# Fillers of TensorE's waits made of 288-column products of zeros, and a new table of due times, in attention followed by two gated MLPs

## The chip, the cores and the metric

The kernel runs on one core of one Trainium2 chip. The metric is the device time of one execution in microseconds (us); the number that counts is the median of the runs timed without the profiler.

## What is computed

Attention over (4, 8, 576, 64) inputs with a window of 32 keys (heads 0 to 3: the last 32 positions; heads 4 to 7: every fourth of the last 128), then a gated MLP with an RMS norm ahead of it, then a second gated MLP. The weights of the MLPs are 512 x 1536 and 1536 x 512.

```python
attn_out = _attn_ref(q, k, v)                       # masked softmax, 4 x 8 heads, 576 positions
x = attn_out.transpose(0, 2, 1, 3).reshape(2304, 512)
xn = x / sqrt(mean(x * x, -1) + 1e-6) * rms_g       # first MLP
x = (silu(xn @ w_gate) * (xn @ w_val)) @ w_out
gate = 1 / (1 + exp(-(x @ w_gate2)))                # second MLP
return (gate * (x @ w_val2)) @ w_out2
```

## The kernel before

**Products.** Every float32 operand of the MLPs is split into two fp32r halves, "hi" and "lo" (`split`, lines 563 to 574), and each product is three TensorE products (hi hi, hi lo, lo hi). The first MLP (`mlp_step` and `y_group`, lines 1264 and 1306) runs over 7 chunks of tokens, `SIZES` = 288 four times and 384 three times, in three passes over the hidden columns. The second MLP (`unit` and `y_products`, lines 1526 and 1444) works on 2 x 2 blocks with seven products in place of eight; VectorE (DVE) and POOL make the sums and differences of blocks.

**Attention.** 48 groups of three 64-query blocks (`attn_group`). A group is: scores on TensorE (line 918, products on quarters of the array), mask and minimum on DVE (line 930), exponentials on ACT (line 936), reciprocal on DVE, a scaling by it on POOL, DVE or ACT, three transposes on TensorE (line 963), a copy, the product with the values (line 976, again on quarters), a copy into `xT`. Twelve groups have to be done ahead of the first chunk; the others are put between the products of the first MLP's first pass. `x_norm` makes the norm of a chunk: squares on ACT, a sum over partitions with `ones` (line 1039), a Newton iteration on DVE or POOL, a copy `rb` on DVE (line 1080), three transposes of it on TensorE (line 1095, `rbp`), the scaling on DVE (line 1107, `xn`), and the split into `xo`. Of chunk 0 all of this lies ahead of the first MLP product.

**Weights.** The inputs hold float64 weights as pairs of 32-bit words. `words` (lines 525 to 561) turns a 128 x 512 block into float32: one ACT instruction into a tile `wz` (line 546), four on DVE (lines 549, 552, 555 and 558). `wz` has 2 buffers. A weight used later is written from `wz` to DRAM (`weight_ahead`, the transfers `z<-wz`) and loaded again when it is due; the buffer is free when that transfer has landed. ACT works in the order given, so an instruction of line 546 that waits for a buffer holds up all of ACT's work behind it.

**The order.** Nothing runs as the code is written. Every piece of work is added to a list with a cost, an engine (or several that may do it) and a due time, and `Line.emit` plays them against a model of the engines: each engine takes the operation that can start first, ties going to the earlier due time. The due times and costs come from the table `PARAMS` (some 120 numbers). The order of instructions on each engine is what the planner writes down; times on the chip may differ from its model.

**Fillers.** Where the planner's model has TensorE wait for more than `fill_from` (0.52 us) ahead of an operation that carries a `fill`, up to a planned time of 330 us, it puts transposes of the identity, 128 columns each, into the bank that the operation will write (`filler`, line 727), as many as its model of TensorE's clock says fit, less `fill_gap`. Their results are never read. At the very start, `warm_up` (line 798) issues 27 products of a tile of zeros with 288 columns. The model of the clock is in `clocked` and `window_at`, with the levels `low` and `high`; products on quarters of the array cost the planner a switch into and out of that mode, and `stay` is what it adds to an operation that would leave it.

## Time and profile before

| | |
|---|---|
| median of 3 runs, not profiled | 1030.18 us (1029.41 to 1032.03) |
| profiled execution, its own time | 1040.96 us |
| its span, first to last instruction | 1039.2 us |
| TensorE (PE) busy | 1001.9 us, 96% |
| DVE busy | 762.0 us, 73% |
| ACT busy | 497.8 us, 48% |
| POOL busy | 381.4 us, 37% |
| mean granted clock of TensorE | 0.978 of 2.4 GHz |

All times in views of the trace are from the start of the span of the profiled execution. "Busy" of TensorE counts from a product's start to its modelled end, so it says little about how well TensorE is used; where products follow each other, the distance from start to start is what one takes. The granted clock has two levels in the records, 1.00 (2.4 GHz) and 0.50 (1.2 GHz); a value between is a stretch with both.

### The profile page before, as it was taken

How to read it: one execution, taken by the hardware profiler on the slowest of the kernel's cores; microseconds unless marked ns; L12 is line 12 of the kernel's file. 1: busy time of each engine (PE TensorE's matmuls, PEld its weight loads, DVE VectorE, ACT ScalarE, POOL GpSimd, SP SyncE). 2: the span in 40 equal slices, each digit the busy share in tenths (PEclk: the TensorE clock that was granted, in tenths of full speed). 3: DMA queues.
4: the chain of work that ended last, by engine and by line, in shares of the span. 5: the costliest groups of instructions: out<-in, count | busy, mean ns of one | idle time of the engine just before them, and what ended most of it. 6: DMA issues, size and time to landing. Idle time of an engine off the chain costs nothing.

```text
span 1039.2 us, 21287 instructions
## 1 busy us (share of the span) xinstructions
PE 1001.9 (96%) x7586; PEld 964.6 (93%) x7586; DVE 762.0 (73%) x1792; ACT 497.8 (48%) x1380; POOL 381.4 (37%) x550
## 2 busy tenths in 40 slices
PE   7989999999999999999999999998999999999997
PEld 6778989899999999999999988998999999999996
DVE  5879877879877677886544576768986679876765
ACT  4848667654553233432322344656653355544432
POOL 4346742545551101301200463426652146632220
PEclk9769999999999999999999999999999999999999
DMA  8749586756889898888876745436254553267642
GB/s 194 169 102 221 128 249 138 165 191 237 296 313 325 313 321 301 276 296 313 287 275 226 248 150 193 176 122 236 74 199 165 226 225 132 100 205 232 173 97 48
DMA packets 207689, 216.62 MB, mean 208 GB/s; under 512 B 136608, under 2 KB 163808, under 8 KB 207584
## 3 DMA queue, kind: packets, MB, share of 16 engines
q1 hardware_dynamic: 207584, 215.27, 64.3%
q8 instruction: 60, 0.98, 0.4%
q14 instruction: 45, 0.37, 0.1%
HBM read 145.23 MB, written 69.99 MB: 207 GB/s over the span
## 4 chain that ended last, share of the span: by engine, by line
PE 66%; DVE 14%; DMA 8%; ACT 4%; issue 4%; POOL 3%; SPq 1%; DVEq 0%; POOLq 0%; ACTq 0%
PE y L1444 11%; PE v L1264 11%; PE y L1306 10%; PE g L1264 10%; PE att L1526 7%; PE v L1526 6%; PE g L1526 4%; DMA xs<-xs 2%; DMA z<-wz 2%; DVE t L1143 2%; PE att L918 2%; DMA wz<-z 2%; POOL w L569 1%; DVE t L1542 1%; DVE S L645 1%
## 5 line engine op out<-in xcount | busy, mean ns | idle before, releaser
L569 POOL TENSOR_TENSOR h<-t,h 128x288 fp32r<-128x288 f32 (+1 forms) x161 | 148.7, 930 | 382.4 <-ACT h L565 350.7
L565 ACT CAST h<-t 128x288 fp32r<-128x288 f32 (+1 forms) x252 | 110.9, 444 | 169.2 <-DVE t L1287 88.0
L1306 PE MATMUL y<-h,wo 128*128 128x288 f32 (+1 forms) x1008 | 174.2, 318 | 0.1
L1264 PE MATMUL g<-xo,w 128*128 128x288 f32 (+1 forms) x1008 | 169.6, 316 | 1.6 <-ACT t L1278 0.5
L1264 PE MATMUL v<-xo,w 128*128 128x288 f32 (+1 forms) x1008 | 167.8, 315 | 0.0
L1444 PE MATMUL y<-h,wo 128*128 128x288 f32 x1008 | 156.0, 297 | 4.9 <-ACT h L565 1.9
L1264 PEld LDWEIGHTS g<-xo,w 128*128 128x128 f32 x1008 | 156.5, 190 | 3.7 <-DVE t L1283 1.0
L1306 PEld LDWEIGHTS y<-h,wo 128*128 128x128 f32 x1008 | 156.2, 190 | 2.8 <-ACT pt L1326 0.2
L1264 PEld LDWEIGHTS v<-xo,w 128*128 128x128 f32 x1008 | 155.6, 190 | 0.8 <-DVE t L1287 0.2
L1444 PEld LDWEIGHTS y<-h,wo 128*128 128x128 f32 x1008 | 141.4, 189 | 7.6 <-ACT h L565 3.0
L1397 DVE SCALAR_TENSOR_TENSOR pt<-y,pt 128x288 f32<-128x288 f32 x136 | 61.5, 453 | 43.5 <-PE y L1444 40.7
L1287 DVE TENSOR_TENSOR t<-t,v 128x288 f32<-128x288 f32 (+1 forms) x84 | 41.3, 491 | 56.7 <-PE v L1264 52.6
L546 ACT ACTIVATE wz<-wst 128x512 f32<-128x512 f32 x72 | 48.1, 669 | 46.4 <-DMA z<-wz 39.5
L1542 DVE TENSOR_TENSOR t<-t,att 128x288 f32<-128x288 f32 x96 | 43.0, 448 | 31.4 <-PE att L1526 28.0
L549 DVE TENSOR_SCALAR wz<-wz 128x512 f32<-128x512 f32 x72 | 35.6, 494 | 39.4 <-ACT wz L546 38.8
L936 ACT ACTIVATE pr<-pr,nmx 128x96 f32<-128x96 f32 x144 | 52.5, 366 | 20.2 <-DVE nmx L930 19.7
L572 DVE TENSOR_TENSOR h<-t,h 128x288 fp32r<-128x288 f32 (+1 forms) x91 | 50.5, 561 | 13.8 <-ACT h L565 11.7
L555 DVE SCALAR_TENSOR_TENSOR wz<-wst,wz 128x512 int32<-128x512 int32 x72 | 57.7, 803 | 1.9
L558 DVE SCALAR_TENSOR_TENSOR wz<-wst,wz 128x512 int32<-128x512 int32 x72 | 58.0, 806 | 1.4
L1278 ACT ACTIVATE t<-g 128x288 f32<-128x288 f32 (+1 forms) x56 | 24.9, 445 | 70.2 <-PE g L1264 70.1
L1526 PE MATMUL att<-xo,w 128*128 128x288 f32 x336 | 54.0, 296 | 1.0 <-DVE t L1143 0.6
L1526 PE MATMUL att<-wst,w 128*128 128x288 f32 x336 | 54.5, 297 | 0.4 <-ACT t L1536 0.4
(210 smaller groups left out, 1787.0 us busy)
## 6 DMA issues: line engine op xcount, KB each, us to landing
z<-wz SPq DMA_DIRECT2D x60, 256.0 KB, 4.5
xo<-xs SPq DMA_DIRECT2D x23, 576.0 KB, 6.8
wst<-in_moe_w_gate_dram SPq DMA_DIRECT2D x24, 512.0 KB, 5.3
wst<-in_moe_w_val_dram SPq DMA_DIRECT2D x24, 512.0 KB, 6.8
wst<-in_moe_w_out_dram SPq DMA_DIRECT2D x24, 512.0 KB, 5.9
xs<-xs SPq DMA_DIRECT2D x21, 576.0 KB, 5.2
wst<-xs SPq DMA_DIRECT2D x18, 576.0 KB, 6.4
xo<-x SPq DMA_DIRECT2D x16, 576.0 KB, 5.4
```

Source lines behind the costliest of these rows:

```text
L555: add("DVE", Shared(0.595), lambda: nc.vector.scalar_tensor_tensor(out=z.t, in0=top(), scalar=-0x40000000, in1=z.t, op0=ALU.bitwise_and, o ...
L558: add("DVE", Shared(0.595), lambda: nc.vector.scalar_tensor_tensor(out=z.t, in0=low(), scalar=29, in1=z.t, op0=ALU.logical_shift_right, op ...
L565: add("ACT", act(n), lambda: nc.scalar.copy(out=hi(), in_=src()), reads=reads, writes=[key] + [order] * bool(order), tiles=tiles + [dst], ...
L569: add("PL", pool(n), lambda: nc.gpsimd.tensor_tensor(out=lo(), in0=src(), in1=hi().bitcast(F32), op=ALU.subtract), reads=reads, writes=[ke ...
L572: other=(kind + "_lo", "DVE", dves(n), lambda: nc.vector.tensor_tensor(out=lo(), in0=src(), in1=hi().bitcast(F32), op=ALU.subtract)))
L936: add("ACT", PARAMS["exp_cost"], lambda u=u: nc.scalar.activation(out=pr.t[:, u], in_=pr.t[:, u], func=ACTF.Exp, bias=nmx.t[:, u:u + 1], s ...
L1264: nc.tensor.matmul(out=bank.t, lhsT=w[:, l, cols], rhs=x[:, r, j], start=kk == 0 and n == 0, stop=kk == KD - 1 and n == 2)
L1306: nc.tensor.matmul(out=yb.t, lhsT=w.t[:, l, s], rhs=h.t[:, r], start=n == 0 and j == 0, stop=n == HOLDS[p] - 1 and j == 2)
L1397: add("DVE", dve(T), lambda: nc.vector.scalar_tensor_tensor(out=t.t[:, e, h], in0=bank.t, scalar=0.5, in1=t.t[:, e, h], op0=ALU.mult, op1= ...
L1444: nc.tensor.matmul(out=bank.t, lhsT=w.t[:, u, a, n], rhs=hs[u].t[:, d], start=first and u == 0 and m == 0, stop=u == NF // 2 - 1 and m == ...
L1526: nc.tensor.matmul(out=bank.t, lhsT=l.t[:, a, cols], rhs=r.t[:, d, j], start=first and j == 0 and m == 0, stop=j == 1 and m == 2, skip_gro ...
L1542: add("DVE", dve(T), lambda: nc.vector.tensor_tensor(out=t.t, in0=t.t, in1=bank.t, op=ALU.add), reads=[(key, uk)], writes=[ck[name]], tile ...
```

## The change

- The filler is now a product of zeros, `[128 x rows]` by `[128 x n]`, with n the columns of the bank it writes, at most 288. The zeros have a tile of their own in the attention stage's memory, used by `warm_up` too.
- Fillers go in until the attention stage's memory is given up (`SWAP`) and no longer until a planned time; `fill_from` is negative, so the length of a wait no longer keeps fillers out: as many whole ones go in as the planned wait less 0.077 us holds.
- A second rule would add fillers without a wait, where the columns of the last stretch are fewer than a share `fill_share`. The table sets that share to -1.645, so that the lack is below zero everywhere and the rule adds nothing.
- `low` and `high` are 0: the planner's model has TensorE at full clock from its first stretch on.
- `wz` has 3 buffers in place of 2; the second MLP's third home for the same blocks, a tile `z` in the later memory, goes, so there are three there as before.
- Nearly all other numbers of the table are new (`stay` from 0 to 0.699 among them), and with them the order on every engine. `late` changes nothing at these sizes.

The diff, the table cut to the lines that are spoken of:

```diff
 PARAMS = {
...
+    "late": 0, "fill_share": -1.645, "fill_max": 6, "gather": -3.359, "w0_hi": 0.17,
...
-    "xb_zero": -1.298, "stay": 0.0, "phase": 1.6, "fill_to": 330.0, "fill_from": 0.52,
+    "stay": 0.699, "phase": 1.6, "fill_from": -2.118, "fill_gap": 0.077, "margin": 2922.227,
...
@@ emit
-            if o.eng == "PE" and o.fill and start < PARAMS["fill_to"]:
+            if o.eng == "PE" and o.fill and not swapped:
                 begin = free["PE"]
...
-                if begin > self.writer["ident"].end and start - begin > PARAMS["fill_from"]:
-                    while True:
-                        self.window_at(int((begin + PARAMS["phase"]) // 3.4133))
-                        step = 0.083 if self.warm else 0.166
-                        if begin + step > start - PARAMS["fill_gap"]:
-                            break
-                        self.clocked(begin, 0.083, 128)
-                        begin += step
-                        o.fills += 1
+                if begin > self.writer["warm"].end:
...
+                    _, step, size = o.fill
+                    gap = start - begin - PARAMS["fill_gap"]
+                    if start - begin > PARAMS["fill_from"]:
+                        o.fills = max(0, int(gap / step))
+                    o.fills += max(0, min(int(lack / size) - o.fills, int(PARAMS["fill_max"])))
...
@@ words
-        z = new("bp", "z", [P, CW], I32, 1) if late else new("sb", "wz", [P, CW], I32, 2)
+        z = new("bp", "z", [P, CW], I32, 1) if late else new("sb", "wz", [P, CW], I32, 3)
...
-    Z_HOMES = (("sb", "wz", 2),) + (("bp", "z", 1),) * (L2P == ONE)
+    Z_HOMES = (("sb", "wz", 3),)
...
@@ filler
+        size = 1
+        for n in bank.shape[1:]:
+            size *= n
+        size = min(size, T)
...
-                nc.tensor.transpose(t[0:rows, 0:P], ident[:, 0:rows], ident)
+                nc.tensor.matmul(out=t[0:rows, 0:size], lhsT=zeros[:, 0:rows],
+                                 rhs=zeros[:, 0:size], start=True, stop=True)
...
+        return fill, 0.0101 + 0.000425 * size, size
```

How the change moves instructions, at three places. In each line stand the line of the kernel (of the changed one: 14 to 16 higher), the operation, the tile written and the tiles read, the shape, and how many follow each other.

TensorE around the norm of chunk 0, ahead of the first MLP product (`y` is here a bank that the attention borrows; `rb` the norm's copy). Before:

```order
L918 MATMUL att<-kT,qT 64x96 x6
L1039 MATMUL v<-ones,pt 96x1 x3
L918 MATMUL att<-kT,qT 64x96 x12
L727 MATMUL y_1144<-ident 128x128 x35
L1095 MATMUL y_1144<-ident,rb 128x96 x3
L1039 MATMUL att<-ones,pt 96x1 x3
L963 MATMUL att<-ident,pr 96x128 x3
L1264 MATMUL g<-xo,w 128x288 x6
```

The same place now:

```order
L932 MATMUL att<-kT,qT 64x96 x12
L1053 MATMUL v<-ones,pt 96x1 x3
L741 MATMUL y_1181<-zeros 128x288 x30
L1109 MATMUL y_1181<-ident,rb 128x96 x3
L1053 MATMUL att<-ones,pt 96x1 x3
L977 MATMUL att<-ident,pr 96x128 x3
L741 MATMUL att<-zeros 128x192 x3
L990 MATMUL att<-pts,v 64x64 x6
L1278 MATMUL g<-xo,w 128x288 x6
L977 MATMUL att<-ident,pr 96x128 x3
L741 MATMUL att<-zeros 128x192 x10
```

30 products of 288 columns stand where 35 transposes of 128 stood, and 13 shorter ones are new around the first MLP product. In all there are 96 fillers for 58: 73 of 288 columns and 23 of 192, all but one of them ahead of the second half of the first MLP product.

ACT at the program's start (`wst` a loaded weight block, `wz` the tile it goes to, `w` the split halves). Before:

```order
L546 ACTIVATE wz<-wst 128x512 x2
L565 CAST w<-wz 128x256 x2
L779 COPY kT<-v 128x288
L779 COPY kT<-g 128x288
L565 CAST w<-wz 128x256
L546 ACTIVATE wz<-wst 128x512
```

Now:

```order
L553 ACT_TABLE_LOAD
L553 ACTIVATE wz<-wst 128x512 x3
L572 CAST w<-wz 128x256 x2
L795 COPY kT<-v 128x288
L795 COPY kT<-g 128x288
L572 CAST w<-wz 128x256 x2
```

The third block no longer stands behind the first block's split: with three buffers its instruction has one of its own.

TensorE in the first pass of the first MLP, third chunk (scores and values, the products on quarters of the array, are the rows with `kT,qT` and with `pts,v`). Before:

```order
L1264 MATMUL g<-xo,w 128x288 x12
L963 MATMUL att<-ident,pr 96x128 x6
L1264 MATMUL v<-xo,w 128x288 x12
L976 MATMUL att<-pts,v 64x64 x6
L918 MATMUL att<-kT,qT 64x96 x6
L1306 MATMUL y_2598<-h,wo 128x288 x3
L918 MATMUL att<-kT,qT 64x96 x12
L1306 MATMUL y_2633<-h,wo 128x288 x3
L1306 MATMUL y_2652<-h,wo 128x288 x3
L976 MATMUL att<-pts,v 64x64 x6
L1306 MATMUL y_2660<-h,wo 128x288 x3
```

Now:

```order
L1278 MATMUL g<-xo,w 128x288 x12
L932 MATMUL att<-kT,qT 64x96 x18
L990 MATMUL att<-pts,v 64x64 x6
L1278 MATMUL v<-xo,w 128x288 x12
L990 MATMUL att<-pts,v 64x64 x6
L977 MATMUL att<-ident,pr 96x128 x3
L1320 MATMUL y_2756<-h,wo 128x288 x3
L977 MATMUL att<-ident,pr 96x128 x3
L1320 MATMUL y_2761<-h,wo 128x288 x3
L990 MATMUL att<-pts,v 64x64 x12
L1320 MATMUL y_2770<-h,wo 128x288 x3
```

The scores of three groups follow each other where there were one and two. From the first MLP product on, TensorE goes over to products on quarters of the array 29 times in place of 47; the scores stand in 14 unbroken pieces in place of 29, the values in 26 in place of 30. The count of products other than fillers is the same.

On the other engines, counted over the whole program: 30 of the subtractions that make the "lo" halves of weights go from DVE to POOL, 14 of the copies that make the "hi" halves from ACT to DVE, and of the 144 scalings by the reciprocal ACT does 52 in place of 15 (DVE 44 for 70, POOL 48 for 59). In the second MLP's last unit the output products (line 1444) now stand one by one between the products of line 1526, where 28 rows of three followed each other.

## Rows read from the trace of the kernel before

**Rows 1.** Busy time and granted clock by stretch: engines' busy us (instructions), PEclk, DMA share, GB/s.

```profile
40.00:60.00 20.00, 20.00 (x188) 16.75 (x187) 13.17 (x59) 13.49 (x48) 5.77 (x12) 0.50 0.43 116
60.00:80.00 20.00, 16.09 (x115) 14.14 (x114) 16.16 (x52) 10.26 (x39) 9.14 (x22) 0.76 0.64 137
80.00:100.00 20.00, 20.00 (x211) 17.59 (x210) 19.79 (x68) 16.41 (x61) 13.47 (x22) 0.92 0.91 208
140.00:160.00 20.00, 17.62 (x172) 15.86 (x172) 14.60 (x58) 13.08 (x49) 7.64 (x13) 0.91 0.85 240
180.00:200.00 20.00, 19.10 (x201) 17.63 (x202) 17.93 (x54) 12.26 (x46) 10.30 (x26) 0.91 0.66 129
```

**Rows 2.** Chain that ended last, from 83 to 200 us: start us, us, what.

```profile
135.59 7.25 DMA z<-wz
142.86 0.67 ACT wz L546
```

**Rows 3.** TensorE in order of time: start us, us, instruction, count [idle before <-releaser].

```profile
145.33 0.71 PE L918 MATMUL att<-kT,qT 64*64 64x96 f32 x12 [0.74 <-DVE xn L1107]
...
148.96 0.71 PE L918 MATMUL att<-kT,qT 64*64 64x96 f32 x12 [0.72 <-DVE nmx L930]
...
151.67 1.22 PE L918 MATMUL att<-kT,qT 64*64 64x96 f32 x12 [0.90 <-DVE nmx L930]
```

**Rows 4.** TensorE in order of time, without waits, at full clock.

```profile
160.60 0.92 PE L976 MATMUL att<-pts,v 96*64 96x64 f32 x24
161.45 0.66 PE L1306 MATMUL y<-h,wo 128*128 128x288 f32 x3
162.04 1.21 PE L918 MATMUL att<-kT,qT 64*64 64x96 f32 x24
163.18 0.65 PE L1306 MATMUL y<-h,wo 128*128 128x288 f32 x3
...
164.50 0.71 PE L918 MATMUL att<-kT,qT 64*64 64x96 f32 x12
165.15 0.57 PE L976 MATMUL att<-pts,v 96*64 96x64 f32 x12
165.65 0.66 PE L1306 MATMUL y<-h,wo 128*128 128x288 f32 x3
166.15 1.75 PE L1264 MATMUL g<-xo,w 128*128 128x288 f32 x12
167.74 0.81 PE L963 MATMUL att<-ident,pr 128*96 128x128 f32 x6
```

**Rows 5.** TensorE in order of time, the fillers ahead of the norm's transposes.

```profile
58.79 5.89 PE L727 MATMUL y<-ident 128*128 128x128 f32 x35
64.51 0.41 PE L1095 MATMUL y<-ident,rb 96*128 96x96 f32 x3
```

**Rows 6.** DVE in order of time, the norm's copy and the first scaling.

```profile
60.25 0.55 DVE L1080 COPY rb<-rsy 96x384 f32<-96x384 f32 x1
...
64.97 0.94 DVE L1107 SCALAR_TENSOR_TENSOR xn<-xT,gam,y 128x288 f32<-128x288 f32 x2 [3.32 <-PE y L1095]
```

**Rows 7.** Busy time and granted clock of one stretch inside the fillers.

```profile
62.00:64.00 2.00, 2.00 (x18) 2.00 (x17) 0.00 (x0) 0.51 (x4) 0.24 (x1) 0.84 0.80 128
```

**Rows 8.** TensorE in order of time, twelve MLP products at half clock.

```profile
79.26 3.25 PE L1264 MATMUL g<-xo,w 128*128 128x288 f32 x12 [0.43 <-DVE t L1283]
82.44 1.01 PE L918 MATMUL att<-kT,qT 64*64 64x96 f32 x12
```

**Rows 9.** TensorE's waits from 320 us on: us in total, times, longest us.

```profile
PE g L1526 <- DVE t L1542: 6.5, 9, 1.6
PE y L1444 <- POOL h L569: 1.8, 3, 1.0
```

**Rows 10.** TensorE in order of time, a wait in the last unit.

```profile
1010.60 1.06 PE L1526 MATMUL g<-xq,w 128*128 128x288 f32 x6 [0.55 <-DVE t L1542]
```

**Rows 11.** TensorE in order of time, the norm's sums over partitions.

```profile
35.76 1.18 PE L1039 MATMUL v<-ones,pt 128*96 128x1 f32 x12
```

More of the change, by code (lines that the diff above doesn't have):

```diff
@@ new lines @@
+    "w0_lo": 1.905, "h0_hi": 0.438, "h0_lo": 1.239, "x0_hi": 1.34, "x0_lo": 11.623, "ahead": 2,
+    "todo0": 56.796, "todo1": 25.362, "todo2": 159.576, "todo3": 11.023, "xb_zero": 1.288,
+    "stay": 0.699, "phase": 1.6, "fill_from": -2.118, "fill_gap": 0.077, "margin": 2922.227,
+    "wait": 1.059, "w_sq": 42.802, "w_hi": 0.161, "w_lo": 1.285, "x_hi": 1.845, "x_lo": 0.0,
+    "h_hi": 1.711, "h_lo": 0.003, "qk": 1.905, "norm": 0.0, "pts": 18.659, "o": 0.0, "snap": 7.898,
+    "h_ahead": 98.614, "h2_ahead": -0.542, "evac": 0.038, "holds": (4, 4, 4), "norm_act": 0.0,
@@ L45 @@
+    "warm_due": 37.022, "mask_cost": 0.18, "exp_cost": 0.36, "s_cost": 0.546, "o_cost": 0.41,
+    "t_cost": 0.265, "pt_lead": 1.847, "x_lead": 29.885, "wy_due": 1.584, "y_from": 5.448,
+    "y_step": 0.787, "xb_due": -0.013, "y_last": 1.205, "xb_last": 0.798, "lo6": 114.943,
+    "hi6": 132.108, "sizes": (288, 288, 288, 288, 384, 384, 384),
 }
@@ L192, in emit @@
         todo = len(self.ops)
-        picks, watch, stale = {}, {}, set(ready)
+        picks, watch, stale, streamed, swapped = {}, {}, set(ready), [], False
         def choose(eng):
@@ L258, in emit @@
                         begin = max(begin, t.ring.free_at() + PARAMS["cross"])
-                if begin > self.writer["ident"].end and start - begin > PARAMS["fill_from"]:
-                    while True:
-                        self.window_at(int((begin + PARAMS["phase"]) // 3.4133))
-                        step = 0.083 if self.warm else 0.166
-                        if begin + step > start - PARAMS["fill_gap"]:
-                            break
-                        self.clocked(begin, 0.083, 128)
-                        begin += step
-                        o.fills += 1
+                if begin > self.writer["warm"].end:
+                    since = start - 3.4133
+                    streamed = [x for x in streamed if x[1] > since]
+                    lack = PARAMS["fill_share"] * 2400 * 3.4133 - sum(
+                        c * min(1.0, (e - since) / (e - s)) for s, e, c in streamed)
+                    _, step, size = o.fill
[3 more added lines that the diff above has]
+                    o.fills += max(0, min(int(lack / size) - o.fills, int(PARAMS["fill_max"])))
+                    if o.fills:
+                        streamed.append((start - step * o.fills, start, size * o.fills))
             self.longer = 0.0
@@ L288, in emit @@
                 cost = self.clocked(start, cost, o.cols)
+                if not swapped:
+                    streamed.append((start, start + cost, o.cols))
             for t in o.tiles:
@@ L293, in emit @@
             if o.fills:
-                o.fill(o.fills)
+                o.fill[0](o.fills)
             fn()
@@ L319, in emit @@
             if o.eng == "SWAP":
+                swapped = True
                 stale.update(ready)
@@ L519, in words @@
         key = (layer, f, i)
-        late = p > L2P and L2P > ONE
+        late = PARAMS["late"] and p > L2P and L2P > ONE
         st = new("bp", "xq", [P, CW, 2], I32, 2) if late else new("sb", "wst", [P, CW, 2], I32, NST)
@@ L787, in warm_up @@
     def warm_up(n, times):
-        z = new("sb", "h", [P, T], F32R, 2)
-        add("PL", 0.3, lambda: nc.gpsimd.memset(z.t.bitcast(F32), 0.0), writes=["warm"],
-            tiles=[z], due=-90)
+        add("PL", 0.3, lambda: nc.gpsimd.memset(zeros.bitcast(F32), 0.0), writes=["warm"], due=-90)
         def some(n, cost, due, release, until=None):
@@ L797, in run @@
                 for _ in range(n):
-                    nc.tensor.matmul(out=bank.t, lhsT=z.t[:, 0:P], rhs=z.t, start=True, stop=True)
-            add("PE", cost, run, reads=["warm"], tiles=[z, bank], due=due, release=release,
+                    nc.tensor.matmul(out=bank.t, lhsT=zeros[:, 0:P], rhs=zeros, start=True, stop=True)
+            add("PE", cost, run, reads=["warm"], tiles=[bank], due=due, release=release,
                 until=until, cols=n * T)
@@ L1686, in whole @@
         for n, (p, f, i) in enumerate(todo):
-            if p > L2P and L2P > ONE:
+            if PARAMS["late"] and p > L2P and L2P > ONE:
                 m = n - [x[0] > L2P for x in todo].index(True)
```

31 lines of the change are left out of this document (11 added, 20 removed), and 6 rows, old and new, of the table PARAMS.

## The prediction

> **What bounds the kernel now.** I read the busy times by stretch first, then the chain that ended last, then TensorE and its neighbours in order of time where the clock or a wait shows. From about 80 us to the end TensorE is the bound: products follow each other from start to start, and what is lost there is a wait, half a clock, or a switch between kinds of products. Ahead of that lies the head, in which attention and the norm of chunk 0 have to be done.
>
> The granted clock shows where time goes beyond the work. From 40 to 60 us it is 0.50 throughout, and 0.76 and 0.92 in the next two stretches; 140 to 160 and 180 to 200 us have 0.91 [rows 1]. As lost clock that is 20 x 0.50 + 20 x 0.24 + 20 x 0.08 = 16.4 us in the head, and twice 20 x 0.09 = 1.8 us later. How much of the 16.4 us was time is another question: from 40 to 60 us ACT is busy for 13.5 and DVE for 13.2 of 20 us [rows 1], so at full clock that stretch could lose at most some 6.5 us before ACT is the bound, and from 80 us on DVE has no room (19.8 of 20).
>
> The sum below is made against the profiled execution, 1040.96 us by its own clock. The median without the profiler is 1030.18, 10.8 less. I cannot place those 10.8 us; the head's lost clock is the one item of that size, so I take it that the timed runs have little of it, and carry a term over to the median only where it doesn't hang on the head's clock.
>
> **The third buffer.** The chain goes through a transfer of a finished weight block, issued at 135.59 and landed 7.25 us later; at 142.86 ACT's next weight block starts, which waited for that buffer [rows 2]. ACT and DVE work in order, so what stood behind was late too: TensorE waits 0.74, 0.72 and 0.90 us for DVE [rows 3], and the clock drops for the 1.8 us counted above. With three buffers the block takes one that was freed a block earlier. 0.74 + 0.72 + 0.90 + 1.8 = 4.16 us go if nothing is late next; nothing goes if another weight instruction is in the way. I take 4.1, the nearer end, since the chain names this transfer and no other in that stretch. ACT has more such waits later, but TensorE doesn't wait there: worth nothing.
>
> **Scores and values gathered.** Two blocks of scores take 163.18 - 162.04 = 1.14 us, one takes 165.15 - 164.50 = 0.65, so the second costs 0.16 less than by itself; of the values two take 0.85 and one 0.50, 0.15 less. A product of three ahead of such a piece takes 0.59 (161.45 to 162.04), elsewhere 0.50 (165.65 to 166.15) [rows 4]. After the first MLP product the change has 15 fewer pieces of scores, 4 fewer of values, and 18 fewer entries: 19 x 0.155 + 18 x 0.09 = 2.9 + 1.6 = 4.5 us of a TensorE that is the bound. Bounds: 0, where DVE, at 19.8 of 20 us from 80 to 100 [rows 1], sets the pace; 4.5 where TensorE does. I take 3.0, because after 100 us DVE is less full and most of the pieces lie there. In the head the same gathering is hidden under ACT and DVE.
>
> **The fillers.** They cost nothing if the planned wait exists at the planned length, and their own length if it doesn't. Twelve products of 288 columns take 167.74 - 166.15 = 1.59 us at full clock [rows 4] and 82.44 - 79.26 = 3.18 at half [rows 8]: 0.133 and 0.265 us each. The dear place is the norm of chunk 0. Its copy is ready at 60.25 + 0.55 = 60.80, but the 35 transposes that began at 58.79 hold TensorE until 64.51, and DVE waits 3.32 us for it [rows 5, 6]; the scaling, the split and the first MLP product all come behind. So the old fillers cost 3.7 us of the chain. Thirty products of zeros would end at 58.79 + 30 x 0.133 = 62.8 at full clock, 1.7 us earlier than now, and at 58.79 + 30 x 0.265 = 66.7 at half, 2.2 later. The two levels have opposite signs, and I take 0 for all fillers, the middle. Ends for the range: -8 us, if the head runs at full clock throughout (6.5 us from ACT's room, plus 1.7), and +11.7, if every filler runs at half clock in a wait cut to full: the 73 long ones 0.132 us over each, the 23 of 192 columns two thirds of that, 9.6 + 2.0. The rule that fills up missing columns adds none, by its share below zero: of the change's two ideas only the longer product acts.
>
> What the clock does with products in place of transposes is open. From 62 to 64 us it reads 0.84, that is it rose to full inside a stretch in which TensorE ran transposes alone [rows 5, 7]; the old fillers could raise it. The Trainium skill says otherwise (TensorE: Matmul & The Clock Gate, Part 4: PE-mode transpose): in transpose mode the engine doesn't count as busy in the same way, and full clock doesn't engage. By that page the old fillers were useless and products are what wakes the clock, so the end of -8 would be the likely one. The trace disagrees with it by the 0.84, so it gets a chance as a rival and no place in the sum.
>
> **The rest of the order.** Behind 320 us TensorE waits 6.5 us for DVE in nine places and 1.8 us for POOL's halves of `h` [rows 9]. Thirty subtractions leave DVE for POOL, which is busy for only 37%, and fourteen copies come to it. I take a quarter of the 6.5, 1.5 us; bounds 0 and 6.5 gain, and 1.8 loss if POOL's halves are late twice as long. In the last unit the output products between those of line 1526 give DVE time, and the 0.55 us wait goes [rows 10]: 0.5. Scalings moved to ACT (37) lie beside TensorE's work, ACT being busy for 48%; without that cover each would delay one group's transposes. Against all this, the order is new everywhere, so waits that the planner doesn't see will stand in new places: 2.0 us, about what one more stretch like [rows 3] costs in waits alone; bounds 0 and 4.2 (with its clock).
>
> **Sum:** -4.1 - 3.0 + 0 - 1.5 - 0.5 + 2.0 = -7.1 us. None of it hangs on the head's clock, so 1040.96 becomes 1033.9, and the median 1030.18 becomes 1023.1.
>
> **Rivals.**
> - *The head runs at full clock.* 73 of the fillers are longer products, and 9 + 3 + 30 of them stand where the trace of before is at half clock the longest. Against it: the clock was at half by 40 us [rows 1], shortly behind 12 products of one column that hold TensorE for 1.18 us [rows 11], and the change keeps those. Then -7.1 - 8 = -15.1: 1015.
> - *Old waits, new places.* The stall at 143 us belongs to one execution, and an order planned with a clock that never falls may lose elsewhere what it saves here. Buffer and order come to nothing together, and the gathering is eaten by DVE: -1 to +2, 1030.5.
> - *The fillers overshoot (slower).* TensorE comes to the waits at half clock, where the planner counted on full, and every filler takes twice its planned time. It decides at the 30 products ahead of the norm: if the clock is at half when they begin, and stays so, `rbp` comes at 66.7 or later. Its price is the +11.7 above, on top of the sum: -7.1 + 11.7 = +4.6, 1035. For it: from 40 to 60 us the trace shows half clock just ahead of this place. Against: 9 + 3 products of 288 columns stand shortly before, and twelve such follow each other at either clock without a gap [rows 4, 8].
> - *The change doesn't do what it says.* It doesn't in one point, as shown: no filler stands where columns run short. That is in the sum already.
>
> **How the numbers follow.** About 0.3%, 3.1 us, is what a measurement of this kernel can tell from no change. Forecast 0.42, its own range 1019 to 1028 (the gathering from 0 to 4.5, the new waits up to 4.2); head at full clock 0.18 (1010 to 1019); old waits, new places 0.21 (1027 to 1033); overshoot 0.19 (1031 to 1040). Faster by over 0.3%, below 1027.1: 0.42 x 0.95 + 0.18 + a little of the third = 0.60. Slower, above 1033.3: 0.19 and a little = 0.21. The rest, 0.19, is the same. The range that leaves out 2 in 10 goes from inside the second case to inside the fourth: 1013 to 1036.
>
> **What would show it.** In the changed profile: no stretch from 130 to 160 us in which ACT's weight instruction waits some microseconds for `z<-wz` while TensorE waits for DVE; pairs and triples of scores at 0.5 us for each block after the first; the norm's transposes within 2 us of its copy `rb` (right for full clock) or 5 behind it (overshoot); the clock at 0.50 for less than the 20 us before 60 (first rival) or not; waits of line 1526 for DVE below 6.5 us. Wrong would be the forecast if the sum of TensorE's waits and lost clock from 84 to 300 us is not at least 3 us smaller than before, or if twelve MLP products first follow each other without a break more than 4 us earlier or later than at 82.44 us [rows 8].

## The result, and the profile after

The changed kernel is slower: 1040.12 us, the median of 11 runs (1036.08 to 1043.91), against 1033.11 (1029.41 to 1038.21) for the kernel before on the same chip, a ratio of 1.0061 with an interval of 1.0038 to 1.0083. (The ratios here are estimates of their own with a 95% interval, and differ by up to 0.14% from the quotient of the two medians.) 1023.1 was forecast. The profiled execution took 1038.41 us, 1.7 below its median; the one of before that the forecast was made against (1040.96) lies above all 11 runs of its kernel. A second profile of the unchanged kernel (run before_again, below: 1032.89 us, near its median) is the fair partner, and is used from here on.

The busy time of the engines in the changed kernel, as the page has it:

```profile
PE 988.2 (95%) x7624; PEld 957.7 (92%) x7624; DVE 737.5 (71%) x1757; ACT 499.6 (48%) x1393; POOL 401.3 (39%) x572
```

TensorE is busy for 13.7 us less than in the first profile of before (7.4 less than in the second), DVE for 24.5 less, and the time is longer than before's median all the same. The rows that answer to [rows 1], in the same columns:

```profile
40.00:60.00 20.00, 18.98 (x253) 16.41 (x254) 16.52 (x87) 17.48 (x69) 8.91 (x19) 1.00 0.49 123
60.00:80.00 20.00, 17.42 (x167) 15.61 (x166) 18.95 (x65) 15.92 (x60) 11.85 (x25) 0.91 0.76 183
80.00:100.00 20.00, 17.99 (x226) 15.96 (x225) 17.69 (x70) 16.75 (x63) 11.29 (x21) 1.00 1.01 201
...
140.00:160.00 20.00, 18.63 (x211) 17.31 (x210) 14.43 (x65) 13.22 (x50) 9.05 (x24) 1.00 0.89 230
```

The same stretches of the second profile of before:

```profile
20.00:40.00 20.00, 18.29 (x225) 14.75 (x223) 16.24 (x88) 17.84 (x73) 8.33 (x17) 0.85 0.87 181
40.00:60.00 20.00, 19.77 (x219) 16.85 (x218) 14.72 (x69) 14.35 (x51) 6.29 (x13) 0.72 0.41 112
60.00:80.00 20.00, 17.50 (x126) 14.68 (x125) 19.41 (x56) 12.12 (x44) 11.39 (x25) 0.74 0.65 142
```

In this execution the change does what it is built for: from 20 to 80 us the clock is full but for 1.8 us' worth, where before loses 20 x (0.15 + 0.28 + 0.26) = 13.8. Little of that was time. And this execution is a favourable one: its mean clock, 0.995, is as high as in any of the 11 runs, whose median is 0.991; for 98 runs of the kernel before, beside the experiments, it is 0.987. So in the usual run the clock won is some 4 us' worth, where these two profiles differ by 10. The table shows where each profiled execution was, counted by the columns that the MLP's products had streamed: the head until 12,000 columns, the attention between the products from there to 300,000, the rest of the first MLP, the second MLP with the end.

| profiled execution | head | attention | first MLP | second MLP | span |
|---|---|---|---|---|---|
| before, first profile | 84.2 | 199.7 | 318.8 | 436.5 | 1039.2 |
| before, second profile | 79.1 | 198.2 | 318.1 | 435.6 | 1031.1 |
| **changed** | 77.5 | 198.8 | 317.9 | 442.1 | 1036.3 |
| changed, second MLP's old numbers | 76.5 | 203.5 | 318.1 | 439.9 | 1037.9 |
| changed, no fillers | 81.2 | 199.5 | 320.2 | 441.8 | 1042.7 |
| changed, transposes as fillers | 81.6 | 201.6 | 317.9 | 445.7 | 1046.8 |
| before, products as fillers | 76.6 | 197.0 | 318.1 | 435.0 | 1026.7 |
| before, third buffer, order kept | 84.3 | 193.3 | 318.1 | 436.1 | 1031.7 |
| before, both of these | 75.1 | 195.6 | 318.1 | 437.5 | 1026.2 |
| before, second MLP's new numbers | 76.5 | 198.8 | 318.0 | 439.4 | 1032.7 |

The head of the changed kernel is 1.6 us shorter than in the second profile of before, the attention the same, the second MLP 6.5 longer.

**The head.** The 30 products of zeros ahead of the norm of chunk 0 (TensorE, then DVE's copy `rb`):

```profile
56.37 4.19 PE L741 MATMUL y<-zeros 128*128 128x288 f32 x30
60.65 0.47 PE L1109 MATMUL y<-ident,rb 96*128 96x96 f32 x3
```

```profile
60.05 0.55 DVE L1094 COPY rb<-rsy 96x384 f32<-96x384 f32 x1
```

They end at 60.56 and the copy at 60.60: no overshoot. The old fillers were 3.7 us too long in the first profile of before [rows 5, 6], but not in the second, nor in the kernel before with the new numbers for the second MLP alone, whose head is in the order of before. The norm's transposes of these two:

```profile
60.77 0.41 PE L1095 MATMUL y<-ident,rb 96*128 96x96 f32 x3
```

```profile
56.99 0.41 PE L1095 MATMUL y<-ident,rb 96*128 96x96 f32 x3
```

There the copy ends at 60.51 and at 56.72, 0.26 and 0.27 us ahead of them. Up to the copy the first of these two heads lost 8.5 us of clock and the second 1.7; the changed kernel lost none by its records, and its copy is as late as the first and 3.9 us later than the second. So the new order of the head is later by itself, and the clock that was won only made that good.

**The attention.** TensorE's waits of a stretch, first the longest in the changed kernel, then in the second profile of before, from 84 to 284 us (us in total, times, longest):

```profile
PE att L932 <- DVE nmx L944: 2.8, 5, 0.8
PE att L932 <- DVE ms L1069: 2.1, 1, 2.1
PE att L1109 <- DVE rb L1094: 1.2, 2, 1.0
```

```profile
PE att L918 <- DVE nmx L930: 1.7, 2, 0.9
PE att L918 <- DVE ms L1055: 0.8, 1, 0.8
PE att L1095 <- DVE rb L1080: 0.4, 1, 0.4
```

All the waits of these two lists, the shorter ones not shown included, add up to 8.6 us now and 4.1 before. The longest, 2.09 us at 115.39, ends this chain of the changed kernel:

```profile
108.87 0.44 SPq L844
109.31 0.05 issue
109.36 0.03 SPq L532
109.39 0.03 issue
109.42 3.95 DMA wst<-in_moe_w_val_dram
113.37 0.02 issue
113.39 0.02 ACTq L553
113.41 0.04 issue
113.45 0.67 ACT wz L553
114.12 0.02 issue
114.14 0.03 DVE wz L556
...
115.27 0.07 DVE ms L1069
```

The load of a weight block is issued behind attention loads (line 844, 0.44 us each on SP) and lands at 113.37. ACT's weight instruction waits for it, DVE's next one waits for ACT, and behind that in DVE's order stands the read of the bank that the gathered scores need. With three buffers ACT's weight instructions wait only 1.8 us for `z<-wz` from 80 to 300 us (two waits, behind 235 us), where they wait 6.8 us in the second profile of before; the load of `wst` is what is late next, at another place.

**The second MLP.** TensorE's products of line 1540 (1526 before) wait for DVE from 500 us on: changed, second profile of before, and the kernel before with the new numbers for the second MLP alone:

```profile
PE g L1540 <- DVE t L1556: 9.2, 8, 2.2
```

```profile
PE g L1526 <- DVE t L1542: 5.9, 10, 1.0
```

```profile
PE g L1526 <- DVE t L1542: 8.8, 8, 2.2
```

The same three first products of a unit wait 2.21, 1.36 and 2.15 us in the changed kernel (at 740.00, 763.19 and 881.51), 0.73, 0.66 and 0.69 in before, 2.23, 1.38 and 2.16 in the third: 3.6 us more. Behind the last of them the clock falls, in the changed kernel, to 0.83 from 880 to 890 us, another 1.7. What is late shows in DVE's order ahead of the first, in the changed kernel and in before (start, us; `t<-t,g` is the sum that frees the bank):

```profile
735.99 0.44 DVE L1556 TENSOR_TENSOR t<-t,att 128x288 f32<-128x288 f32 x1
736.35 0.45 DVE L1157 TENSOR_TENSOR t<-t,t 128x288 f32<-128x288 f32 x1
736.72 1.02 DVE L652 TENSOR_TENSOR S<-wz,S 128x256 f32<-128x256 f32 x1
737.67 1.01 DVE L652 TENSOR_TENSOR S<-wz 128x256 f32<-128x256 f32 x1
738.60 0.98 DVE L1157 TENSOR_TENSOR t<-t,t 128x288 f32<-128x288 f32 x1
739.50 0.44 DVE L1556 TENSOR_TENSOR t<-t,g 128x288 f32<-128x288 f32 x1
```

```profile
734.25 1.02 DVE L645 TENSOR_TENSOR S<-wz,S 128x256 f32<-128x256 f32 x1
...
736.11 0.44 DVE L1542 TENSOR_TENSOR t<-t,att 128x288 f32<-128x288 f32 x1
736.47 0.63 DVE L1143 TENSOR_TENSOR t<-t,t 128x288 f32<-128x288 f32 x1
737.02 1.02 DVE L645 TENSOR_TENSOR S<-wz 128x256 f32<-128x256 f32 x1
737.97 0.44 DVE L1542 TENSOR_TENSOR t<-t,g 128x288 f32<-128x288 f32 x1
738.34 0.68 DVE L1143 TENSOR_TENSOR t<-t,t 128x288 f32<-128x288 f32 x1
```

The block sum `S<-wz,S` stands ahead of the freeing sum in both, only later now. What is new ahead of it is one sum of halves (738.60, 0.90 us from start to start), which stood behind it before (738.34). From the sum `t<-t,att` that starts at 731.38 now and at 731.31 before, DVE takes 8.12 us to the freeing sum for 6.66: 0.90 for the sum of halves, and 0.56 because the instructions that both have take longer together.

In all, TensorE's waits in the second MLP are 17.2 to 18.9 us in the four profiles with its new numbers and their order kept (the changed kernel, the two runs on its fillers and the run with the new second MLP alone), and 13.1 to 15.5 in the nine with the old numbers and their order kept.

### The profile page after: what moved, and what is told of

It is laid out like the page before. It is cut to its first block, busy times and chain, and to the rows that moved or that the text cites. A ratio compares the mean times of both kernels' runs of the same rounds, so it can differ in the third digit from the quotient of the medians.

```text
span 1036.3 us, 21382 instructions
## 1 busy us (share of the span) xinstructions
PE 988.2 (95%) x7624; PEld 957.7 (92%) x7624; DVE 737.5 (71%) x1757; ACT 499.6 (48%) x1393; POOL 401.3 (39%) x572
## 4 chain that ended last, share of the span: by engine, by line
PE 73%; DVE 14%; ACT 5%; DMA 3%; issue 2%; POOL 2%; SPq 1%; DVEq 0%; POOLq 0%; ACTq 0%
PE y L1320 13%; PE v L1278 13%; PE g L1278 13%; PE y L1458 11%; PE att L1540 8%; PE v L1540 6%; PE g L1540 5%; DVE t L1157 2%; ACT pr L950 2%; DVE t L1556 2%; PE att L932 1%; DVE h L579 1%; PE att L990 1%; DVE S L652 1%; DVE t L1578 1%
## 5 line engine op out<-in xcount | busy, mean ns | idle before, releaser
L1320 PE MATMUL y<-h,wo 128*128 128x288 f32 (+1 forms) x1008 | 169.6, 315 | 0.3 <-ACT pt L1340 0.2
L1278 PE MATMUL g<-xo,w 128*128 128x288 f32 (+1 forms) x1008 | 166.7, 313 | 0.0
L1458 PE MATMUL y<-h,wo 128*128 128x288 f32 x1008 | 158.9, 298 | 5.8 <-ACT h L572 1.9
L950 ACT ACTIVATE pr<-pr,nmx 128x96 f32<-128x96 f32 x144 | 52.2, 365 | 11.6 <-DVE nmx L944 11.5
L562 DVE SCALAR_TENSOR_TENSOR wz<-wst,wz 128x512 int32<-128x512 int32 x72 | 55.8, 778 | 1.4
L565 DVE SCALAR_TENSOR_TENSOR wz<-wst,wz 128x512 int32<-128x512 int32 x72 | 55.6, 773 | 1.1
L1157 DVE TENSOR_TENSOR t<-t,t 128x288 f32<-128x288 f32 x82 | 52.6, 642 | 1.3 <-POOL h L576 0.7
```

The costliest lines, as they stand in the source:

```text
L562: add("DVE", Shared(0.595), lambda: nc.vector.scalar_tensor_tensor(out=z.t, in0=top(), scalar=-0x40000000, in1=z.t, op0=ALU.bitwise_and, o ...
L950: add("ACT", PARAMS["exp_cost"], lambda u=u: nc.scalar.activation(out=pr.t[:, u], in_=pr.t[:, u], func=ACTF.Exp, bias=nmx.t[:, u:u + 1], s ...
L1157: add("DVE", dves(n), lambda: nc.vector.tensor_tensor(out=dst(), in0=a(), in1=c(), op=ALU.subtract), reads=reads, writes=writes, tiles=til ...
L1278: nc.tensor.matmul(out=bank.t, lhsT=w[:, l, cols], rhs=x[:, r, j], start=kk == 0 and n == 0, stop=kk == KD - 1 and n == 2)
L1320: nc.tensor.matmul(out=yb.t, lhsT=w.t[:, l, s], rhs=h.t[:, r], start=n == 0 and j == 0, stop=n == HOLDS[p] - 1 and j == 2)
L1458: nc.tensor.matmul(out=bank.t, lhsT=w.t[:, u, a, n], rhs=hs[u].t[:, d], start=first and u == 0 and m == 0, stop=u == NF // 2 - 1 and m == ...
```

## The experiments

Theories: A, the new numbers of the second MLP cost; B, the fillers do by being too long; C, fillers or attention do; D, the head's order does; E, fillers are what holds either head; F, the change's code does; G, scalings moved to ACT set the head's end; H, they don't. (In the first expectation A and B stand for something else, said there.)

**before_again**, the kernel before as it is.

> The kernel before, unchanged, to see another profile of it. In the profile shown of it the head (to 80 us) has half clock from 40 to 60 us and the first MLP product at full speed comes at 82.4 us. Theory A (that profile's head is an exception; the timed runs of before have their head at full clock, and the change's gain there is none in the median): a span some 5 to 8 us shorter than 1039.2, the first MLP products some 4 to 8 us earlier than 82.4, and from 300 us to the end the same pace as in the profile shown. Theory B (the head is always so): a span within 2 us of 1039.2 and the products at the same times.

Measured: 1033.27 beside 1031.95 (ratio 1.0003, 0.9974 to 1.0032), profile 1032.89. Between the two theories of that text: the span is 8.1 us shorter than in the first profile (head 5.0, attention 1.5, the rest 1.6), yet the head is at half clock for much of its length again. So the 10.8 us between the first profile and the median were not the head's clock alone, and an execution near the median can have half clock in the head.

**after_old_second**, the changed kernel with the numbers of before for the second MLP, set where its due times are written and, for `margin` and `wait`, where the memory is handed over:

```diff
-        at = end + 2.1
+        PARAMS.update({'w0_hi': 0.18, ...}); at = end + 2.1
```

> The changed kernel with the table of before for the second MLP alone (due times and engine penalties from the end of the first MLP on); fillers, buffers and attention as changed. The change against before was +7 us. In the two profiles the second MLP gave back 5.5 us (from 7.6 ahead at 500 us to 1.9 ahead at 988). Theory A (the second MLP's new order is the cost): 4 to 6 us faster than the changed kernel, so about 1034 to 1036. Theory C (fillers or attention are the cost): within 1.5 us of the changed kernel, 1039 to 1041.

Measured: 1035.35 beside 1031.95 (1.0030, 1.0006 to 1.0054). 1.0061 becomes 1.0030: half of the loss, a step that the two intervals by themselves just fail to tell from none. The time is inside theory A's range and outside C's. The first-product waits at the three places are 0.73, 0.66 and 0.69 us again. Its profile's attention is 4.7 us longer than that of the changed kernel, though the orders there are the same. The clock was at half there for 10.2 us from 115.0 and 183.2 us on, 5.1 us' worth, where the changed kernel's profile lost none; the first fall comes right behind the wait that was 2.09 us long in the changed kernel:

```profile
PE att L932 <- DVE ms L1069: 2.8, 1, 2.8
```

**before_new_second**, the other way round: the kernel before with only the new numbers for the second MLP, by the same line.

```diff
-        at = end + 2.1
+        PARAMS.update({'w0_hi': 0.17, ...}); at = end + 2.1
```

> The kernel before with the changed table for the second MLP alone. The changed kernel with the old table there came out at 1035.35 (before beside it 1031.95), some 3.5 us faster than the changed kernel against its before. Theory A (the new table costs by itself in the second MLP): 3 to 5 us slower than before, ratio 1.003 to 1.005, with longer waits of the gate products for DVE's t (5.9 us in ten places in the last profile of before). If it costs only behind the new attention stage: within 1 us of before.

Measured: 1037.82 beside 1033.88 (1.0045, 1.0020 to 1.0069), 4.6 us by the ratio and 3.9 by the medians, with the waits shown above. This interval leaves out 1; theory A holds for this part, both ways.

**after_nofill**, the fillers not issued, the order kept:

```diff
-                o.fill[0](o.fills)
+                pass
```

> The changed kernel without its 96 fillers, the order of everything else the same. Theory B (the fillers overshoot in the timed runs): up to 11 us of TensorE's work goes, the time falls by 4 to 8 us, to about 1032 to 1036, and the first MLP product comes no later. Theory A: the fillers lie in waits; without them the time is the same within 2 us, if the clock does not need them, or 3 to 8 us longer, if without them the head falls to half clock.

Measured: 1043.10 beside 1031.95 (1.0094, 1.0059 to 1.0130), 0.33% or 3.4 us slower than with them. Theory B, which expected 4 to 8 us less time, falls; the 3.4 us themselves lie inside the two intervals, but the profiles' heads differ by as much (81.2 for 77.5). The clock drops to 0.70 and 0.67:

```profile
20.00:40.00 20.00, 16.02 (x185) 13.21 (x185) 13.80 (x72) 18.46 (x68) 6.00 (x13) 0.70 0.96 182
40.00:60.00 20.00, 18.20 (x204) 15.36 (x202) 13.22 (x70) 15.40 (x58) 6.39 (x14) 0.67 0.43 117
```

and at the norm TensorE simply waits, with nothing in its place (65.04 for 60.65):

```profile
65.04 0.74 PE L1109 MATMUL y<-ident,rb 96*128 96x96 f32 x3 [3.57 <-DVE rb L1094]
```

**after_transposes**, each filler as transposes of the identity of about as many columns:

```diff
-            for _ in range(n):
-                nc.tensor.matmul(out=t[0:rows, 0:size], lhsT=zeros[:, 0:rows], ...)
+            for _ in range(round(n * size / P)):
+                nc.tensor.transpose(t[0:rows, 0:P], ident[:, 0:rows], ident)
```

> The changed kernel with each filler of n columns as n/128 transposes of the identity, as the kernel before has them, in the same places; about the same number of columns streamed. If products keep the clock up where transposes do not, the head shows 10 us or more at half clock and the time is 3 to 8 us longer than the changed kernel (1043 to 1048). If the kind of filler does not matter, the clock and the time are those of the changed kernel within 2 us.

Measured: 1046.63 beside 1031.95 (1.0133, 1.0101 to 1.0164). The time is as expected for the first case, the reason is not: the clock stays at 1.00, and the transposes follow each other at 0.11 us, as the 35 in the second profile of before do at full clock (56.90 to 60.77).

```profile
20.00:40.00 20.00, 17.46 (x254) 15.45 (x251) 13.86 (x73) 17.79 (x68) 5.37 (x12) 1.00 0.94 179
40.00:60.00 20.00, 18.40 (x273) 16.19 (x268) 15.98 (x85) 18.27 (x70) 8.66 (x19) 1.00 0.50 123
```

```profile
58.44 7.62 PE L741 MATMUL y<-ident 128*128 128x128 f32 x68
65.90 0.41 PE L1108 MATMUL y<-ident,rb 96*128 96x96 f32 x3
```

68 transposes take 7.46 us, 0.110 each of 128 columns, where 30 products took 4.2, 0.14 each of 288. A transpose held TensorE nearly twice as long per column; here that makes `rbp` 3.3 us late behind a copy that was ready at 62.64, 2.0 us later than in the changed kernel by itself.

**before_nofill** and **before_products**: the kernel before without its transposes, and with products of zeros in their places, the order kept in both.

```diff
-                o.fill(o.fills)
+                pass                                  # before_nofill
...
-            for _ in range(n):
-                nc.tensor.transpose(t[0:rows, 0:P], ident[:, 0:rows], ident)
+            size = min(t.shape[1], T)                 # before_products
+            for _ in range(round(n * P / size)):
+                nc.tensor.matmul(out=t[0:rows, 0:size], lhsT=zeros[:, 0:rows], ...)
```

> The kernel before without its 58 filling transposes, everything else in the same order. The last profile of before has 13.8 us of lost clock between 20 and 80 us all the same (granted clock 0.85, 0.72, 0.74), so its fillers do little for the clock. Theory D (the changed order of the head costs more than its fillers give): the old order needs no fillers, time within 2 us of before, 1030 to 1034, far below the 1043.1 of the changed kernel without fillers. Theory E (fillers are what holds either head): 5 us or more slower than before.

> The kernel before with its 58 transposes replaced, in the same places, by products of zeros of about the same number of columns (some 27 products). In the changed kernel products in place of transposes were worth 6 us (1040.1 to 1046.6 against their befores). Theory E: 2 to 6 us faster than before, 1026 to 1030. Theory D (few and short fillers, the order is what counts): within 1.5 us of before.

Measured: without, 1036.03 beside 1033.88 (1.0022, 0.9991 to 1.0054): no clear difference, runs from 1030.3 to 1045.1, so D is as expected and E's 5 us or more are only just possible. With products, 1030.98 beside 1033.88 (0.9971, 0.9947 to 0.9995), and a second time:

> The kernel before with its 58 transposes as some 27 products of zeros, a second time, since its interval (0.9947 to 0.9995) nearly reaches 1: if the gain is real, a ratio of 0.995 to 0.999 again; if it was chance, 0.999 to 1.002.

1031.37 beside 1032.92 (0.9977, 0.9953 to 1.0001). Two runs agree on 0.23 to 0.29%, some 2.4 to 3 us; this beats both kernels, if by little (the second interval reaches just past 1). More of them do not help: **products_plus** adds three ahead of each of nine pieces of scores.

```diff
+            o.fills += 7 * (o.eng == "PE" and o.quad and o.cols == 1152 and 28 < start < 50)
             if o.fills:
```

> The kernel before with its fillers as products of zeros (1030.98 against 1033.88), and three more products of 288 columns ahead of each of nine pieces of scores between 28 and 50 us of the planner's time, where the profiles of that order show TensorE's products at half speed (35 to 48 us). If the half clock there holds up the head: 1 to 3 us faster than with the products alone, 1028 to 1030, the products of the head at full speed throughout. If the head's end hangs on ACT and DVE there: the same within 1 us. If the added products hold TensorE back: 1 to 3 us slower.

Measured: 1032.29 beside 1032.96 (0.9991, 0.9971 to 1.0011), and the head still at 0.83 from 40 to 80 us.

**after_code_old_table**, all of the change's code, the old numbers with these of the new ones:

```diff
-    "low": 0.32, "high": 0.365,
+    "low": 0, "high": 0, "late": 0, "fill_share": -1.645, "fill_max": 6,
```

> All of the change's code (product fillers to the end of attention, three buffers for weight blocks, a planner that takes the clock for full) with the numbers of the old table in everything else, fill_from 0.52 included. Theory A and D together (the code helps, the new numbers of the table cost): as fast as before or faster by up to 5 us, 1027 to 1032. Theory F (the code itself costs, by fillers and by a planner blind to the clock): 3 to 8 us slower than before, 1035 to 1040.

Measured: 1043.46 beside 1033.88 (1.0083, 1.0056 to 1.0111), slower than even theory F expected; head 75.7, second MLP 436.6, but attention 208.4, with 6.8 us' worth of clock lost from 219 us on. A planner that counts on other clock writes another order, and its attention falls behind. So the change's code without its table loses too, and no run has the new table with the old code. The next three show the same and more.

**old_second_less_act**, **before_more_act**, **before_wz3**: one number of the table or one buffer changed (the first on top of after_old_second), the order written anew.

```diff
-                    ("norm_act", "ACT", 0.28,                                # old_second_less_act
+                    ("norm_act0" if start else "norm_act", "ACT", 0.28,      # norm_act0: 0.308
...
-    "norm_act": 0.308,                                                   # before_more_act
+    "norm_act": 0.0,
...
-    Z_HOMES = (("sb", "wz", 2),) + (("bp", "z", 1),) * (L2P == ONE)         # before_wz3
+    Z_HOMES = (("sb", "wz", 3),)
```

> The changed kernel with the old table for the second MLP (1035.35 before), and with scaling on ACT in the first twelve groups made as dear for the planner as in the kernel before (0.308 for 0.0). ACT's list ahead of the first silu then has 7 scalings for 15 and 9 rounded halves for 13. In the profiles the changed head runs at full clock and still reaches its first MLP product at 62.3 to 63.6 us, with ACT busy for 60.5 us of them; the old order at full clock reaches it at 59.6 to 60.5 with ACT busy for 55 to 57. Theory G (ACT sets the head's end, and the instructions moved to it cost their length there): first MLP product 2 to 4 us earlier, at 59 to 61 us, and the time 1031 to 1034. Theory H (ACT is only a symptom): first product within 1 us of 62.3 to 63.6.

> The kernel before with the price of scaling on ACT alone set to 0.0 as in the change: the planner puts 15 scalings for 3 on ACT ahead of the first silu, and the order behind moves with it. Theory G: first MLP product 1 to 3 us later than in the kernel before at the same clock, and 2 to 5 us slower in all. Theory H: within 1.5 us of before.

> The kernel before with three buffers for finished weight blocks (and without the third home later), its table otherwise as it was; the planner orders anew. The prediction gave this part -4.1 us. In the second profile of before ACT waits just as long for that transfer (6.8 us from 80 to 300), but no clock falls from 140 to 160 us. If the buffer is worth what was predicted: 3 to 4 us faster, 1028 to 1030. If the stall was one execution's: within 2 us of before.

Measured: 1056.90, 1049.67 and 1053.58 beside 1032.96 (1.0235, 1.0153, 1.0196). Their attention takes 227.0, 217.1 and 215.7 us: each new order loses 17 to 29 us there, which hides any part. One thing can still be read: before_more_act had 11 scalings on ACT ahead of its first MLP product for none, 4.1 us of ACT, and reached that product at 58.98 and 12,000 columns at 71.5, earlier than any other. old_second_less_act had 4 there for the changed kernel's 8 and reached its first product at 63.78, no earlier than the changed kernel (63.57). Theory G, that ACT sets the head's end, falls. (ACT is busy for 44.8 us ahead of that product in the changed kernel and for 41.7 in the second profile of before, not for 60.5 and 55 to 57, as the expectation has it.) What makes the changed head late is open.

**wz3_kept** and **products_wz3_kept**: three buffers in memory, the planner still counting on two and one later, so that the order stays:

```diff
+        if tag in ("wz", "z"):
+            return Tile(ring, lambda: pools["sb"].tile(shape, dt, tag="wz", name="wz", bufs=3))
```

> The kernel before with three buffers in memory for finished weight blocks, while the planner still counts on two (and the later third home): the order of instructions is that of before, only the wait for the transfer z<-wz can go. The run with a new order for three buffers says nothing on the buffer, since the new order lost 15 us at one place by itself. If the wait of ACT for that transfer costs what the prediction gave it: 3 to 4 us faster than before. If it was covered, but for one execution: within 1.5 us of before, with ACT's waits for z<-wz (6.8 us from 80 to 300 in the second profile of before) gone all the same.

> The kernel before with product fillers in place of its transposes, and three buffers as in the run beside this one, the order of instructions kept. If both help on their own: 3 us from the products (1030.98 to 1033.88 in the run before) and the buffer's part on top, 1026 to 1030. If the buffer is worth nothing: the same as with the products alone, ratio 0.995 to 0.999.

Measured: 1030.62 and 1030.82 beside 1032.92 (0.9976, 0.9956 to 0.9996; 0.9976, 0.9957 to 0.9995). The buffer alone is worth some 2.5 us, by an interval that nearly reaches 1. ACT's waits for `z<-wz`, in the second profile of before

```profile
ACT wz L546 <- DMA z<-wz: 6.8, 4, 3.0
```

are gone from 80 to 300 us, and TensorE's waits from 84 to 284 us add up to 1.4 us for 4.1. With products on top it gains no more in the median; why the two don't add is open.

## Why the prediction was wrong

1. **The profile it was made against.** "I take it that the timed runs have little of" the head's lost clock: wrong. The second profile, near the median, has 13.8 us of it; the first one's excess lay in all stages (5.0, 1.5, 1.6). So the room for fillers was there in the median too. Besides, the 1030.18 that the sum was carried to is the median of three runs; eleven give 1033.11.
2. **Third buffer, -4.1.** The wait was real and the sign right: -2.5 with the order kept. Of the four numbers summed, the 1.8 us of clock was one execution's; the second profile has 1.00 from 140 to 160. But the condition "if nothing is late next" failed in the new order: 2.09 us at 115.39 for the load of `wst`.
3. **Gathering, -3.0.** In the windows from 80 to 260 us the products of scores fell from 21.66 us (376 of them) to 19.72 (365), 0.058 to 0.054 each, 1.3 us in all; those of the values stayed at 0.043 to 0.044. A price was named with the bound 0 (DVE sets the pace) and not taken in full: scores wait for DVE to empty their bank, 2.8 and 2.1 us in the rows above, for 1.7 and 0.8 in the second profile of before (part of the 8.6 us in step 5).
4. **Fillers, 0.** Better than that: some 3.4 us gained by them in the new order, a size that the intervals leave open. Their length was right (4.2 us for 4.0 forecast, `rbp` 0.05 us behind `rb`). The 3.7 us that the old ones cost were the first profile's; in the second they cost 0.26. The rival that gave the head full clock had the clock right, but not the price: the head is 1.6 us shorter, not 8. It ends with the norm, whose last step ahead of TensorE is DVE's copy, and in the new order that copy ends at 60.60 at full clock, where the old order has it at 56.72 with 1.7 us of clock lost. For this the prediction has no term (of the head's gathering it says "hidden under ACT and DVE"), and it took back what the clock gave. The overshoot, which forecast 1035, came nearest by its time and is refuted by its place: that is luck. That transposes don't engage the clock (the Trainium skill, TensorE: Matmul & The Clock Gate, Part 4: PE-mode transpose) no run bears out: with 198 of them as fillers among other products the clock stayed at 1.00, through 7.46 us of transposes alone as well.
5. **The rest of the order, -1.5, the last unit, -0.5, new waits, +2.0.** This is the step that failed: together it put the new order at nothing. It counted on a quarter of the 6.5 us of waits for DVE going, for subtractions that leave DVE; they rose to 9.2 instead, 3.6 of it in three places with a clock's fall behind the last, and the run that does this part alone is 4.6 us slower. The new waits in attention were given 2.0 us with a bound of 4.2; they came to 8.6 us where an old order with the same buffer has 1.4. Only the 0.55 us wait of the last unit did go. (The subtractions that left DVE for POOL are 22 of weights net by the traces, not 30, and 11 copies came to it, not 14.)

The sum as the profiles have it, changed against the old order with products and three buffers (the same two ideas without the new table): head +2.4, attention +3.2, first MLP -0.2, second MLP +4.6, together 10.1 us of span. (The profile of the old order is 2.8 us faster than the median of its runs, the changed one 1.7.) By the ratios much the same comes out: the two ideas in the old order give 0.0024, the change loses 0.0061, so the new order (the table, with a planner that counts on full clock) costs some 0.0085, 8.8 us. The second MLP's part is shown by runs both ways; that the attention's 3.2 is the waits for DVE is read from the rows and wasn't undone by itself; the head's 2.4 is no more than the spread of heads with products in the old order (75.1 to 79.5).

Of the signs that the prediction named, the waits for `z<-wz` are gone from 130 to 160 us, scores follow each other at 0.5 us, `rbp` is within 2 us. The waits of line 1526 for DVE, which were to fall below 6.5 us, rose to 9.2. Both signs of a wrong forecast came true: waits and lost clock from 84 to 300 us are 8.6 + 0 for 4.2 + 3.6, not 3 smaller; and the first `g` of twelve products begins at 75.17 for 79.26, over 4 us earlier, though only 0.7 against the 75.88 of the second profile.

## What to carry to other kernels

When a table of numbers decides the order, its new order is a part of the change with a price of its own, and has to be forecast stage by stage: here parts worth 2 to 3 us each were lost in an order 9 to 10 us worse. To measure one part, change memory or instructions and keep the order; with the order written anew, one number or one buffer moved the time by 16 to 21 us here, far more than the part. And take a second profile of the kernel before, if the first lies outside its timed runs.

## What the runs showed of the hardware

**A clock of 1.00 that was none.** In the profile of before_nofill the granted clock reads 1.00 from 20 to 70 us, but four transposes of 72 columns take as long as at half clock in the second profile of before (there 0.42 at full, 0.69 at half). First the window and one row of before_nofill, then two rows of before:

```profile
20.00:40.00 20.00, 19.17 (x178) 14.91 (x178) 13.34 (x68) 16.12 (x60) 6.47 (x13) 1.00 1.04 195
```

```profile
34.01 0.69 PE L768 MATMUL g<-ident,pt 72*128 72x72 f32 x4
```

```profile
29.66 0.42 PE L768 MATMUL g<-ident,pt 72*128 72x72 f32 x4
...
39.97 0.69 PE L768 MATMUL g<-ident,wo 72*128 72x72 f32 x4
```

Its products ran at that half speed up to some 70 us. The first record of the clock in that trace stands at 73.58 us (in the second profile of before at 16.95, in the changed kernel's at 18.77), and where there is no record the view has 1.00. So a mean clock of 0.993 stands beside both 1030.30 and 1045.06 us among its runs. Durations of one known form tell the level; the column alone doesn't.

**What half clock costs hangs on where it falls.** In the changed order the head without fillers lost 20.5 us of clock and took 81.2 us, with them 1.7 and 77.5: 3.7 us for 18.8. In the order of before, with its transposes, heads that lost 6.8, 13.7, 17.1 and 17.1 us took 76.5, 79.1, 84.2 and 84.3: 7.8 us for 10.3, part of it the fillers' overshoot in the last two. And of the 98 timed runs of the kernel before beside the experiments, the 24 with a mean clock of 0.990 or more have a median of 1030.3 us, the 17 with 0.982 or less one of 1037.1: 6.8 us for some 11.5 us' worth of clock. That the clock is the cause in those runs, and not a sign of waits that cost time by themselves, is not shown.
